# Two column blocks of w2 in sixteen small early transfers, w2's end in parts of 4, 3 and 1, and a reordered head: a decode block of attention beside a Mish layer on one core

## The chip, the cores and the metric

The kernel runs on one core of a Trainium2 chip. The metric is the device time of one execution in microseconds (us), as the median of several executions. A profile is taken from one execution; its "span" reaches from the first to the last recorded instruction and is a little shorter than the execution's own time. The core has five engines with a queue of instructions each: TensorE (PE, with its weight loads as PEld), VectorE (DVE), ScalarE (ACT), GpSimd (POOL) and SyncE (SP). Transfers between HBM and the on-chip memory SBUF are issued by SP or by ACT and carried by 16 DMA engines.

## The reference

One decode step for 8 sequences (B = 8) of width D = 512. After a layer norm, grouped-query attention with 32 query heads on 8 key/value heads over a cache of 8192 positions, and a dense layer with Mish of width F = 1792, are computed side by side and added to the input:

```python
xn = _layernorm(x)
q = (xn @ wq)                      # 8 x 32 heads x 128
scores = q . k_cache * 128**-0.5   # cache: 8 x 8 x 8192 x 128, float32
o = softmax(scores) . v_cache
h = xn @ w1 + b1
act = h * tanh(softplus(h))
out = x + o @ wo + act @ w2
```

Everything is float32. The two caches are 268 MB each, so the execution reads 561 MB.

## The kernel before

**Units.** The work is cut into 32 units (`UNITS`); a unit is one sequence and two key/value heads. Each unit needs one transfer of 8.4 MB from the key cache (`k_t`, laid out as `kT`) and one of 8.4 MB from the value cache (`v_t`). Eight units with the same pair of heads make a group; wq comes in four parts of 2 MB, one per group, into the tile `ws`.

**Places in SBUF.** One tile `kv` of 160 KB per partition holds everything large: values at `V_AT`, keys alternately at the two places `K_AT`. Before the first keys arrive in the first key place, x, its centred copy `xc`, the bias b1 and some small tiles lie there, and w1 is loaded into that place. After the last unit wo (four parts) and w2 take the place of the values and the keys.

**The order.** All instructions are first recorded in a `Program`; `solve` finds which must wait for which, and `emit` writes them out. Every engine runs its own in the order of the source. PE and DVE run units 1 to 30 as a loop of 15 turns with two units each; SP, ACT and POOL are written out without a loop. All large transfers are issued by SP, one after the other; x and b1 alone are issued by ACT. A transfer that PE waits for has its own semaphore.

**The head.** DVE first clears four PSUM banks (H, O, M, A) and makes the small selection matrices (`perm`, `gsum`, `mask` and so on), and only then the layer norm of x. PE multiplies x into bank A, transposes `xc` (four pieces) and the reordered copy `xd` (eight pieces) into bank M. When they are done, SP issues w1 and then the second unit's keys. `project(0, ...)` then multiplies by wq in two halves of eight matmul instructions, each followed by a copy on ACT and four transposes on PE.

**The end.** `parts` cuts w2, seen as 128 rows of 56 column blocks (a block is 512 B of a row), into six transfers: 16, 16, 8, 8, 6 and 2 blocks. PE takes the four parts of wo (`outputs`), the first two parts of w2 (`down_wide`, into bank A) and the others block by block (`down`, into bank H); ACT copies A between, PE adds it to H, DVE copies H to `os`, and SP stores it.

```python
w2_rows = w2.rearrange("j p f -> (j p) f").rearrange("(q i) f -> q (i f)", i=W2R)
parts = ((0, 16), (16, 32), (32, 40), (40, 48), (48, 54), (54, 56))
for lo, hi in parts:
    t = kv[:, W2_AT + lo * P : W2_AT + hi * P]
    nc.sync.dma_start(t, w2_rows[:, lo * P : hi * P])
```

Of the kernel before, what the change touches and what calls it, by code (L numbers as in the profile page):

```python
# [14 lines left out]
P = 128  # L15
B = 8
# [9 lines left out]
G = 4  # L26
# [37 lines left out]


LOAD_Q, MAKE_Q, SPREAD_Q = 4, 5, 7

FIRST, TURNS = 1, (UNITS - 2) // 2
HEAD = mybir.EngineType.DVE
# [356 lines left out]
def kernel(  # L426
# [94 lines left out]
    make_identity(nc, ident)  # L521
    nc.gpsimd.memset(ones, 1.0)
    nc.gpsimd.memset(pt8, 0.0)
    for t in (H, O, M, A):
        nc.vector.memset(t, 0.0)
    for d in range(2):
        nc.vector.tensor_copy(
            perm.rearrange("p (d k c h) -> p d k c h", d=2, c=2, h=REP)[:, d],
# [2 lines left out]
    nc.vector.reduce_sum(  # L531
        gsum, ident.rearrange("p (x g q) -> p g x q", g=4, q=PP), axis=AX.XY
    )
    nc.vector.reduce_sum(mask, ident.rearrange("p (x d) -> p x d", x=NB), axis=AX.X)
    nc.vector.reduce_sum(bsel, ident.rearrange("p (g q) -> p q g", g=G), axis=AX.X)
    nc.vector.reduce_sum(
        isel, ident.rearrange("p (c t h) -> p t c h", t=TL, h=H2), axis=AX.XY
# [1 line left out]
    for d in range(2):  # L539
# [2 lines left out]
            ident.rearrange("p (c d k h) -> p d h c k", c=2, d=2, h=REP)[:, d],  # L542
            axis=AX.XY,
        )
    nc.vector.reduce_sum(
        wide[:, 0], ident.rearrange("p (g i) -> p g i", g=DG), axis=AX.X
    )
    nc.vector.tensor_copy(
        wide[:, 1:], wide[:, 0:1].to_broadcast([P, NB - 1, DG])
    )  # L550
    nc.vector.reduce_sum(dsel, ident.rearrange("p (g i) -> p i g", i=DI), axis=AX.X)
    nc.vector.reduce_sum(
        fsel, ident.rearrange("p (c h g) -> p h c g", h=2, g=2 * W1R), axis=AX.XY
    )
    nc.vector.reduce_sum(usel, ident.rearrange("p (q i) -> p i q", i=WOR), axis=AX.X)
    nc.vector.reduce_sum(
        qsel[:, :Q], ident.rearrange("p (q i) -> p q i", i=WOR), axis=AX.X
# [9 lines left out]
        .to_broadcast([G, 2, 2, B]),  # L567
    )


    st = const.tile([B, 8], F32, name="st")
    nc.vector.reduce_sum(st[:, 0:1], x_sb, axis=AX.X)
    nc.vector.tensor_scalar_mul(st[:, 1:2], st[:, 0:1], 1.0 / D)
    nc.vector.tensor_scalar(xc, x_sb, st[:, 1:2], None, op0=ALU.subtract)
    nc.scalar.activation(sq, xc, AF.Square, accum_out=st[:, 2:3])
    nc.vector.tensor_scalar(
        st[:, 3:4], st[:, 2:3], 1.0 / D, EPS, op0=ALU.mult, op1=ALU.add
    )
    nc.scalar.activation(st[:, 4:5], st[:, 3:4], AF.Sqrt)
    nc.vector.reciprocal(st[:, 5:6], st[:, 4:5])  # L580
    nc.vector.tensor_mul(st[:, 6:7], st[:, 5:6], st[:, 5:6])
    nc.vector.tensor_mul(st[:, 7:8], st[:, 6:7], st[:, 3:4])
    nc.vector.tensor_scalar(st[:, 6:7], st[:, 7:8], -0.5, 1.5, op0=ALU.mult, op1=ALU.add)
    nc.vector.tensor_mul(st[:, 4:5], st[:, 6:7], st[:, 5:6])
    nc.vector.tensor_scalar(xc, xc, st[:, 4:5], None, op0=ALU.mult)
    nc.tensor.matmul(A[:B, :], ident[:B, :B], x_sb, start=True, stop=False)
    for c in range(CC):
        nc.tensor.transpose(M[:, c * B : (c + 1) * B], xc[:, c::CC], ident[:B, :B])
    nc.vector.tensor_copy(xn4.rearrange("p c b -> p (c b)"), M[:, 0:32])
    xd = kv[:B, W1_AT + 3 * D : W1_AT + 5 * D].rearrange("p (i k) -> p i k", i=W1R)  # L590
    for h in range(2):
        nc.vector.tensor_copy(
            xd.rearrange("p i (c h g) -> p h i c g", c=CC, h=2)[:, h],
            xc.rearrange("p (c g i) -> p i c g", c=CC, i=W1R),
        )
    for i in range(W1R):
        nc.tensor.transpose(
            M[:, 32 + i * B : 32 + (i + 1) * B], xd[:, i], ident[:B, :B]
        )
    for h in range(2):  # L600
        nc.vector.tensor_scalar(
            xnT[:, :, h],
            M[:, 32 : 32 + W1R * B].rearrange("p (i b) -> p i b", i=W1R),
            fsel[:, h : h + 1],
            None,
            op0=ALU.mult,
        )

    def project(m, qp):

        nc.tensor.take("wq")
        w = ws.rearrange("p (c f) -> p c f", c=CC)
        for d in range(2):
            for c in range(CC):
                nc.tensor.matmul(
                    H[:B, :],
                    xn4[:, c, :],
                    w[:, c, d * 512 : (d + 1) * 512],
                    start=(c == 0),
                    stop=(c == CC - 1),  # L620
                )
            nc.scalar.copy(qp[:B], H[:B]).tell("qp")
            nc.tensor.take("qp")
            for h in range(REP):
                at = 192 + (d * REP + h) * B
                made = nc.tensor.transpose(
                    M[:, at : at + B], qp[:B, h * DH : (h + 1) * DH], ident[:B, :B]
                )
        made.tell("tq")
        qT = ws[:, 2 * BW : 2 * BW + H2 * B]  # L630
        nc.vector.take("tq")
        nc.vector.tensor_scalar_mul(qT, M[:, 192 : 192 + H2 * B], DH**-0.5).tell("q")
        return qT
# [64 lines left out]
        if part == 1:  # L698
            made.tell("s")

    def softmax(j):
        nc.vector.take("s")
        nc.vector.relay()
        nc.vector.tensor_reduce(nm, S, axis=AX.X, op=ALU.max, negate=True).tell("nm")
        nc.tensor.take("nm")
        nc.tensor.transpose(M[:1, 0:P], nm, ident).tell("mt")
        nc.vector.take("mt")
        row = M[:1, 0:P].rearrange("p (c d k h) -> p d h c k", c=2, d=2, h=REP)
        for d in range(2):
            low_max = nc.vector.tensor_reduce(nr[:, d], row[:, d], axis=AX.XY, op=ALU.min)  # L710
        low_max.tell("nr")
        nc.vector.take("nr")
        for c in range(2):
            wide_max = nc.vector.tensor_copy(
                nx[:, c],
                nr.rearrange("p d (o h) -> p d o h", o=1).to_broadcast([1, 2, NH * G, REP]),
            )
        wide_max.tell("nx")
        nc.tensor.take("nx")
        nc.tensor.transpose(  # L720
            M[:, 128:129], nx.rearrange("p c d k h -> p (c d k h)"), ident[:1, :1]
        ).tell("xt")
        nc.vector.take("xt")
        nc.vector.tensor_copy(nmx, M[:, 128:129])
        nc.scalar.activation(es[j % 2], S, AF.Exp, bias=nmx, accum_out=l).tell("e")
# [97 lines left out]

    hp = H[:, :FG]

    def hidden(w1_t, b1_sb):
        for i in range(W1R):
            for n in range(2):
                nc.tensor.matmul(
                    hp[Q * n : Q * n + 2 * B, :],  # L830
                    xnT[:, i].rearrange("p h b -> p (h b)"),
                    w1_t[:, i, n * FG : (n + 1) * FG],
                    start=(i == 0),
                    stop=False,
                )
        for n in range(2):
# [96 lines left out]
    def down(lo, hi, w):  # L933
        for n in range(lo, hi):
            j, g = divmod(n, G)
            nc.tensor.matmul(
                H[Q * g : Q * g + B, :P],
                aT[:, j, :],
                w[:, (n - lo) * P : (n - lo + 1) * P],
                start=(n < parts[2][0] + G),  # L940
                stop=(j == 2 * W2R - 1),
            )


    nc.sync.dma_start(
        kv[:, W1_AT : W1_AT + W1R * W1F],
        w1.rearrange("j p f -> (j p f)").rearrange("(p f) -> p f", p=P),
    )
    qT = project(0, es[0])
    k_t[1] = load_unit(kT, 1, K_AT[1])  # L950
    mask_queries(qT)
    spread()
    key_weights(0)

    w2_rows = w2.rearrange("j p f -> (j p) f").rearrange("(q i) f -> q (i f)", i=W2R)
    v_t = {}
    for j in range(UNITS):
        b = j % B
# [16 lines left out]
        softmax(j)  # L975
        if b == 0 and j > 0:
            with nc.only("sums"):
                sums()
# [15 lines left out]
            load_q(j // B + 1)  # L994
        if more and b == MAKE_Q:
            with nc.only("make"):
                qT = project(j // B + 1, es[(j + 1) % 2])
                mask_queries(qT)
        turn(j, late)
        if j == 0:  # L1000
            hidden(w1_t, b1_sb)
        if j > 0:
            merge(j - 1)
    sums()
    nc.turn = None

# [7 lines left out]
            .rearrange("(p f) -> p f", p=P),  # L1014
        )
    w2_t = []
    parts = ((0, 16), (16, 32), (32, 40), (40, 48), (48, 54), (54, 56))
    for lo, hi in parts:
        t = kv[:, W2_AT + lo * P : W2_AT + hi * P]
        nc.sync.dma_start(t, w2_rows[:, lo * P : hi * P])  # L1020
# [6 lines left out]
    turn_masked(NP - 1, es[0])  # L1027
    turn_rows(NP - 1)
    outputs(NP - 1, w_o[NP - 1])
    down_wide(*parts[0], w2_t[0])  # L1030
    down_wide(*parts[1], w2_t[1])
    down(*parts[2], w2_t[2])
# [58 lines left out]
```

## Time and profile before

| | us |
|---|---|
| median of 3 executions | 1303.69 (1303.64 to 1304.04) |
| the profiled execution | 1303.81 |
| its span | 1302.0 |
| PE busy | 912.2 (70%) |
| DVE busy | 399.5 (31%) |
| ACT busy | 43.1 (3%) |
| queue of SP's transfers, share of 16 DMA engines | 99.6% |

How the page is read: the busy time of an engine is a mean over the whole execution. The line called DMA cuts the span into 40 slices and gives the busy share of the 16 DMA engines in tenths (9 is 90% or more). The chain of waits goes back from the last instruction to what released it. A view by windows gives the same sums for stretches that one chooses, and the list of DMA queues can be asked for any stretch, down to one that holds a single packet; its last number is the time that the packets starting there took, as a share of 16 engines over that stretch. It can be above 100% where packets reach beyond the stretch.

### The profile page before, as it was taken

The numbers are of one execution on the slowest core, as the hardware profiler recorded it, in microseconds if no ns is written. First come the engines' busy times: TensorE is split into PE (matmuls) and PEld (weight loads), VectorE is DVE, ScalarE is ACT, GpSimd is POOL, SyncE is SP. The second block draws the span as 40 slices with busy tenths as digits, with TensorE's granted clock in tenths as the row PEclk, the third lists the DMA queues.
The fourth block names the chain that finished last, engine by engine and source line by source line (L and its number), as shares of the span: only waits on it lengthen the run. The fifth ranks groups of instructions, "written<-read, shape, count | busy, mean of one in ns | idle before, by whom it ended". The sixth has DMA issues, their size and how long they took to land. (4 is left out here: it accounts for less than half of the span.)

```text
span 1302.0 us, 11473 instructions
## 1 busy us (share of the span) xinstructions
PE 912.2 (70%) x4570; PEld 297.8 (23%) x4570; DVE 399.5 (31%) x874; ACT 43.1 (3%) x104; POOL 1.7 (0%) x8
## 2 busy tenths in 40 slices
PE   4877767668766668775678666677576667666667
PEld 1222222222222222222222222222222222222121
DVE  3332233431333331233321333322333331333431
ACT  2000000000000000000000000000000000000000
POOL 0000000000000000000000000000000000000000
PEclk9899778898788788888887877798887798788788
DMA  9999999999999999999999999999999999999998
GB/s 400 452 422 441 427 437 433 435 433 431 439 427 443 425 445 425 443 425 445 425 443 427 443 427 441 429 435 433 433 437 433 435 429 441 427 443 425 443 418 351
DMA packets 11555, 561.22 MB, mean 431 GB/s; under 512 B 1292, under 2 KB 1552, under 8 KB 1944
## 3 DMA queue, kind: packets, MB, share of 16 engines
q1 hardware_dynamic: 11520, 561.06, 99.6%
q8 instruction: 6, 0.10, 0.0%
q14 instruction: 5, 0.04, 0.0%
q10 hardware_dynamic: 24, 0.02, 0.0%
HBM read 561.01 MB, written 0.07 MB: 431 GB/s over the span
## 5 line engine op out<-in xcount | busy, mean ns | idle before, releaser
L378 PE MATMUL s<-kv,wk 128*64 128x512 f32 x2048 | 515.7, 667 | 226.2 <-PEq L365 226.2
L378 PEld LDWEIGHTS s<-kv,wk 128*64 128x64 f32 x2048 | 174.5, 154 | 550.0 <-issue 550.0
L378 PE MATMUL o<-kv,pt 128*32 128x512 f32 x2048 | 268.1, 683 | 22.7 <-PEq L365 22.3
L378 DVE TENSOR_REDUCE nm<-s 128x1 f32<-128x512 f32 x32 | 22.1, 692 | 479.5 <-DVEq L365 479.5
L378 PEld LDWEIGHTS o<-kv,pt 128*32 128x32 f32 x2048 | 81.5, 123 | 183.1 <-issue 182.7
L378 DVE TENSOR_SCALAR os<-o,isel 128x128 f32<-128x128 f32 x32 | 11.2, 351 | 287.7 <-DVEq L365 287.7
L378 DVE STREAM_TRANSPOSE tr<-x 128x512 f32<-128x512 f32 x128 | 80.0, 682 | 1.3 <-DVEq L365 1.3
L378 DVE TENSOR_TENSOR wk<-qr,mask 128x512 f32<-128x512 f32 x64 | 61.8, 1007 | 8.9 <-DVEq L365 6.4
L378 DVE SCALAR_TENSOR_TENSOR pt<-tr,gsum,y 64x256 f32<-64x256 f32 x128 | 56.2, 479 | 5.2
L378 ACT ACTIVATE e<-s,nmx 128x512 f32<-128x512 f32 x32 | 22.0, 687 | 1046.1 <-DVE nmx L378 1046.1
L378 DVE SCALAR_TENSOR_TENSOR y<-tr,gsum,y 128x512 f32<-128x512 f32 x64 | 48.3, 755 | 9.4
L378 DVE SCALAR_TENSOR_TENSOR os<-o,isel,os 128x128 f32<-128x128 f32 x96 | 33.7, 351 | 14.1 <-DVEq L365 0.3
L378 PE MATMUL x<-e,perm 128*128 128x512 f32 x64 | 36.5, 653 | 1.4 <-PEq L365 1.3
L378 PE MATMUL m<-ident,nm 128*1 128x128 f32 x32 | 8.6, 269 | 32.2 <-PEq L365 32.2
L378 PE MATMUL h<-ws,xn 128*8 128x512 f32 x64 | 30.5, 622 | 0.0
L378 PE MATMUL m<-ident,nx 1*128 1x1 f32 x32 | 6.4, 200 | 34.2 <-PEq L365 34.2
L378 PE MATMUL t<-ident,os 128*128 128x128 f32 x32 | 9.6, 299 | 26.6 <-PEq L365 26.6
L378 DVE TENSOR_SCALAR y<-tr,gsum 128x512 f32<-128x512 f32 x32 | 24.1, 754 | 1.2
L378 DVE TENSOR_REDUCE nr<-m 1x4 f32<-1x64 f32 x64 | 11.0, 207 | 18.1 <-DVEq L365 18.1
L378 PEld LDWEIGHTS m<-ident,nm 128*1 128x1 f32 x32 | 2.5, 79 | 59.5 <-issue 59.5
L378 PEld LDWEIGHTS x<-e,perm 128*128 128x128 f32 x64 | 10.0, 192 | 24.1 <-issue 23.7
L378 PEld LDWEIGHTS t<-ident,os 128*128 128x128 f32 x32 | 4.5, 140 | 46.6 <-issue 46.6
(91 smaller groups left out, 154.1 us busy)
## 6 DMA issues: line engine op xcount, KB each, us to landing
ws<-in_wq SPq DMA_DIRECT2D x4, 2048.0 KB, 32.6
kv<-in_wo SPq DMA_DIRECT2D x4, 2048.0 KB, 24.4
kv<-in_w SPq DMA_DIRECT2D x1, 3584.0 KB, 22.0
kv<-in_w SPq DMA_DIRECT2D x2, 1024.0 KB, 32.0
kv<-in_w SPq DMA_DIRECT2D x2, 512.0 KB, 33.8
kv<-in_kT SPq DMA_DIRECT2D x32, 29.1
kv<-in_v SPq DMA_DIRECT2D x32, 29.4
kv<-in_w SPq DMA_DIRECT2D x1, 384.0 KB, 34.7
```

Of the source, the lines that this page charges most:

```text
L378: ins = getattr(engine, op.method)(*[here(x) for x in op.args], **{k: here(x) for k, x in op.kw.items()})
```

## The change

1. In units 24 to 31, after `merge`, ACT issues two small transfers per unit, 16 in all. They carry blocks 32 and 33 of w2 (1 KB per row) into a free part of `ws`, in 15, 14, ... 1 and at last 8 rows. PE takes these two blocks in a `down` of its own ahead of the first `down_wide`.
2. The parts of w2 at the end are now 16, 16, 6, 8, 4, 3 and 1 blocks.
3. The head is reordered. The layer norm comes ahead of most selection matrices, with a first activation that has ACT load the table for the square root; the transposes of `xd` (now `turn_x`, into bank X) stand inside `project(0, ...)`, between its matmuls and its transposes; the two halves of wq's product use two banks and two tiles; x is multiplied into bank A after `project`; and `hidden` (the product with w1) is spread over the first unit's softmax. SP's w1 transfer stands behind all of `project(0, ...)` and behind the matmul into A. A `project` in the loop keeps its order.

```diff
+EARLY = (32, 34)
+EARLY_ROWS = tuple(range(15, 0, -1)) + (8,)
+EARLY_AT = UNITS - B
...
-    for t in (H, O, M, A):
-        nc.vector.memset(t, 0.0)
+    st = const.tile([B, 8], F32, name="st")
+    nc.scalar.activation(st[:, 0:1], ident[:B, :1], AF.Sqrt)
+    nc.vector.memset(M, 0.0)
+    nc.vector.reduce_sum(st[:, 0:1], x_sb, axis=AX.X)
...
-    def project(m, qp):
+    def project(m, qps, banks, fill=None):
...
+        products(0)
+        if fill is not None:
+            products(1)
+            fill()
+            turned(0)
+        else:
+            turned(0)
+            products(1)
+        turned(1).tell("tq")
...
-                start=(n < parts[2][0] + G),
+                start=(n < EARLY[0] + G),
...
+    def turn_x():
+        for i in range(W1R):
+            nc.tensor.transpose(X[:, i * B : (i + 1) * B], xd[:, i], ident[:B, :B])
...
+    qT = project(0, es, (H, Y), turn_x)
+    nc.tensor.matmul(A[:B, :], ident[:B, :B], x_sb, start=True, stop=False)
     nc.sync.dma_start(
         kv[:, W1_AT : W1_AT + W1R * W1F],
         w1.rearrange("j p f -> (j p f)").rearrange("(p f) -> p f", p=P),
     )
-    qT = project(0, es[0])
...
+    w2_early = ws[:, 3 * BW : 3 * BW + (EARLY[1] - EARLY[0]) * P]
...
+        if j == 0:
+            softmax(j, hidden)
+            hidden(4, 6)
+        else:
+            softmax(j)
...
+        if j >= EARLY_AT:
+            for n in range(2 * (j - EARLY_AT), 2 * (j - EARLY_AT + 1)):
+                rows = slice(sum(EARLY_ROWS[:n]), sum(EARLY_ROWS[: n + 1]))
+                nc.scalar.dma_start(w2_early[rows], w2_rows[rows, EARLY[0] * P : EARLY[1] * P])
...
-    parts = ((0, 16), (16, 32), (32, 40), (40, 48), (48, 54), (54, 56))
+    parts = ((0, 16), (16, 32), (34, 40), (40, 48), (48, 52), (52, 55), (55, 56))
...
+    down(*EARLY, w2_early)
     down_wide(*parts[0], w2_t[0])
```

More of the change, by code (lines that the diff above doesn't have):

```diff
@@ L523 @@
     nc.gpsimd.memset(pt8, 0.0)
-    for t in (H, O, M, A):
-        nc.vector.memset(t, 0.0)
+    st = const.tile([B, 8], F32, name="st")
+    nc.scalar.activation(st[:, 0:1], ident[:B, :1], AF.Sqrt)
+    nc.vector.memset(M, 0.0)
+    nc.vector.reduce_sum(st[:, 0:1], x_sb, axis=AX.X)
+    nc.vector.tensor_scalar_mul(st[:, 1:2], st[:, 0:1], 1.0 / D)
+    nc.vector.tensor_scalar(xc, x_sb, st[:, 1:2], None, op0=ALU.subtract)
+    nc.scalar.activation(sq, xc, AF.Square, accum_out=st[:, 2:3])
+    nc.vector.memset(H, 0.0)
+    nc.vector.reduce_sum(dsel, ident.rearrange("p (g i) -> p i g", i=DI), axis=AX.X)
+    nc.vector.tensor_scalar(
+        st[:, 3:4], st[:, 2:3], 1.0 / D, EPS, op0=ALU.mult, op1=ALU.add
+    )
+    nc.scalar.activation(st[:, 4:5], st[:, 3:4], AF.Sqrt)
+    nc.vector.reduce_sum(
+        wide[:, 0], ident.rearrange("p (g i) -> p g i", g=DG), axis=AX.X
+    )
+    nc.vector.reciprocal(st[:, 5:6], st[:, 4:5])
+    nc.vector.tensor_mul(st[:, 6:7], st[:, 5:6], st[:, 5:6])
+    nc.vector.tensor_mul(st[:, 7:8], st[:, 6:7], st[:, 3:4])
+    nc.vector.tensor_scalar(st[:, 6:7], st[:, 7:8], -0.5, 1.5, op0=ALU.mult, op1=ALU.add)
+    nc.vector.tensor_mul(st[:, 4:5], st[:, 6:7], st[:, 5:6])
+    nc.vector.tensor_scalar(xc, xc, st[:, 4:5], None, op0=ALU.mult)
+    for c in range(CC):
+        nc.tensor.transpose(M[:, c * B : (c + 1) * B], xc[:, c::CC], ident[:B, :B])
+    nc.vector.tensor_copy(xn4.rearrange("p c b -> p (c b)"), M[:, 0:32])
+    nc.vector.tensor_copy(
+        wide[:, 1:], wide[:, 0:1].to_broadcast([P, NB - 1, DG])
+    )
+    nc.vector.reduce_sum(mask, ident.rearrange("p (x d) -> p x d", x=NB), axis=AX.X)
+    xd = kv[:B, W1_AT + 3 * D : W1_AT + 5 * D].rearrange("p (i k) -> p i k", i=W1R)
+    for h in range(2):
+        nc.vector.tensor_copy(
+            xd.rearrange("p i (c h g) -> p h i c g", c=CC, h=2)[:, h],
+            xc.rearrange("p (c g i) -> p i c g", c=CC, i=W1R),
+        )
+    nc.vector.reduce_sum(
+        fsel, ident.rearrange("p (c h g) -> p h c g", h=2, g=2 * W1R), axis=AX.XY
+    )
+    nc.vector.memset(A, 0.0)
+    nc.vector.memset(O, 0.0)
     for d in range(2):
@@ L533 @@
     )
-    nc.vector.reduce_sum(mask, ident.rearrange("p (x d) -> p x d", x=NB), axis=AX.X)
     nc.vector.reduce_sum(bsel, ident.rearrange("p (g q) -> p q g", g=G), axis=AX.X)
@@ L544 @@
         )
[L545 to L554, printed above, removed]
     nc.vector.reduce_sum(usel, ident.rearrange("p (q i) -> p i q", i=WOR), axis=AX.X)
@@ L568, with products @@
     )
[L571 to L607, printed above, removed]
-    def project(m, qp):
+    def project(m, qps, banks, fill=None):
         nc.tensor.take("wq")
         w = ws.rearrange("p (c f) -> p c f", c=CC)
-        for d in range(2):
+        def products(d):
             for c in range(CC):
                 nc.tensor.matmul(
-                    H[:B, :],
+                    banks[d][:B, :],
                     xn4[:, c, :],
@@ L621, in project, with turned @@
                 )
-            nc.scalar.copy(qp[:B], H[:B]).tell("qp")
+            nc.scalar.copy(qps[d][:B], banks[d][:B]).tell("qp")
+        def turned(d):
             nc.tensor.take("qp")
@@ L626, in project @@
                 made = nc.tensor.transpose(
-                    M[:, at : at + B], qp[:B, h * DH : (h + 1) * DH], ident[:B, :B]
+                    M[:, at : at + B], qps[d][:B, h * DH : (h + 1) * DH], ident[:B, :B]
                 )
-        made.tell("tq")
+            return made
+        products(0)
[7 more added lines that the diff above has]
+        turned(1).tell("tq")
         qT = ws[:, 2 * BW : 2 * BW + H2 * B]
@@ L699, in scores, with softmax @@
             made.tell("s")
-    def softmax(j):
+    def softmax(j, fill=lambda lo, hi: None):
         nc.vector.take("s")
@@ L704, in softmax @@
         nc.vector.tensor_reduce(nm, S, axis=AX.X, op=ALU.max, negate=True).tell("nm")
+        fill(0, 2)
         nc.tensor.take("nm")
@@ L718, in softmax @@
         wide_max.tell("nx")
+        fill(2, 4)
         nc.tensor.take("nx")
@@ L824, with hidden @@
     hp = H[:, :FG]
-    def hidden(w1_t, b1_sb):
-        for i in range(W1R):
+    def hidden(lo, hi):
+        for i in range(lo, hi):
             for n in range(2):
@@ L835, in hidden @@
                 )
+        if hi < W1R:
+            return
         for n in range(2):
@@ L939, in down @@
                 w[:, (n - lo) * P : (n - lo + 1) * P],
-                start=(n < parts[2][0] + G),
+                start=(n < EARLY[0] + G),
                 stop=(j == 2 * W2R - 1),
             )
+    def turn_x():
+        for i in range(W1R):
+            nc.tensor.transpose(X[:, i * B : (i + 1) * B], xd[:, i], ident[:B, :B])
+        for h in range(2):
+            nc.vector.tensor_scalar(
+                xnT[:, :, h],
+                X[:, : W1R * B].rearrange("p (i b) -> p i b", i=W1R),
+                fsel[:, h : h + 1],
+                None,
+                op0=ALU.mult,
+            )
+    qT = project(0, es, (H, Y), turn_x)
+    nc.tensor.matmul(A[:B, :], ident[:B, :B], x_sb, start=True, stop=False)
     nc.sync.dma_start(
@@ L974 @@
         scores(j, k, j % 2 == 0, 1)
-        softmax(j)
+        if j == 0:
[3 more added lines that the diff above has]
+            softmax(j)
         if b == 0 and j > 0:
@@ L996 @@
             with nc.only("make"):
-                qT = project(j // B + 1, es[(j + 1) % 2])
+                qT = project(j // B + 1, [es[(j + 1) % 2]] * 2, (H, H))
                 mask_queries(qT)
@@ L1000 @@
         if j == 0:
-            hidden(w1_t, b1_sb)
+            hidden(6, W1R)
         if j > 0:
             merge(j - 1)
+        if j >= EARLY_AT:
+            for n in range(2 * (j - EARLY_AT), 2 * (j - EARLY_AT + 1)):
+                rows = slice(sum(EARLY_ROWS[:n]), sum(EARLY_ROWS[: n + 1]))
+                nc.scalar.dma_start(w2_early[rows], w2_rows[rows, EARLY[0] * P : EARLY[1] * P])
     sums()
```

## The prediction

> **What bounds the kernel now.** I read the page first, for what is busy from end to end; then the chain of waits, for what ends last; then windows over the last microseconds.
>
> ```profile
> span 1302.0 us, 11473 instructions
> ...
> DMA  9999999999999999999999999999999999999998
> ...
> q1 hardware_dynamic: 11520, 561.06, 99.6%
> ```
>
> ```profile
> 1263.61 34.75 DMA kv<-in_w
> ...
> 1298.40 0.74 PE h L378 x15
> ...
> 1299.16 0.29 DVE os L378
> ```
>
> The 16 DMA engines are full in every slice, 99.6% of the span by SP's queue alone. The last instruction hangs on w2's last transfer, which lands at 1298.35. So the time is: start, plus the bytes of the DMA engine that ends last over its rate, plus what follows the landing. An edit counts only if it leaves the DMA engines dry, changes the load of the engine that ends last, or shortens what follows.
>
> ```profile
> 2.00:26.00 24.00, 13.08 (x38) 3.67 (x38) 8.73 (x36) 4.46 (x7) 0.70 (x1) 1.00 1.04 436
> 60.00:1250.00 1190.00, 838.13 (x4173) 276.37 (x4169) 367.62 (x793) 33.11 (x85) 0.00 (x0) 0.84 1.00 434
> 1297.00:1297.56 0.56, 0.23 (x11) 0.13 (x11) 0.00 (x0) 0.00 (x0) 0.00 (x0) 1.00 0.15 57
> 1297.56:1298.01 0.45, 0.45 (x16) 0.20 (x8) 0.00 (x0) 0.00 (x0) 0.00 (x0) 1.00 0.05 20
> 1298.01:1298.36 0.35, 0.04 (x4) 0.00 (x0) 0.00 (x0) 0.00 (x0) 0.00 (x0) 1.00 0.07 23
> ```
>
> The last two columns are the DMA engines' busy share and GB/s. The rate is 434 to 436 GB/s in the head and in the long middle: there is no hole to fill. At the end the engines stop one by one: 0.15 x 16 = 2.4 are at work until 1297.56, and from there on 0.05 x 16 = 0.8 and 0.07 x 16 = 1.1, so **one engine alone** for the last 0.8 us. That straggler sets the end.
>
> **The change, part by part.** First the price of a packet (one row of a transfer on one DMA engine).
>
> ```profile
> q10 hardware_dynamic: 4, 0.01, 3.7%
> q1 hardware_dynamic: 8, 0.01, 6.0%
> q1 hardware_dynamic: 1, 0.07, 1511.2%
> ```
>
> These are rows of the list of DMA queues, asked for three stretches in turn. In 5.80 to 6.30 ACT's queue brings b1: 4 packets of 1.8 KB, 0.037 x 16 x 0.5 = 0.30 us, 0.074 each. In 1298.015 to 1298.36 the straggler works alone on seven rows of 1 KB and a word that counts the transfer: 0.06 x 16 x 0.345 = 0.331 us, about 0.046 a row and 0.009 the word. In 60.17 to 60.18 one key packet of 65,536 B starts: 15.112 x 16 x 0.01 = 2.418 us, 0.0378 per KB. So a packet takes 0.008 + 0.0378 per KB: 0.159 for 4 KB, 0.121 for 3, 0.084 for 2, 0.065 for 1.5, 0.046 for 1, 0.027 for 0.5.
>
> *Removed and added at the end.* Each engine carries 8 of the 128 rows. Before, the parts of 8, 6 and 2 blocks cost it 8 x (0.159 + 0.121 + 0.046) = 2.61 us. After, 6, 4, 3 and 1 blocks cost 8 x (0.121 + 0.084 + 0.065 + 0.027) + 0.01 for one more count = 2.39. **Term 1: -0.22 us** on every engine alike.
>
> *Added before.* These bytes still have to come, and in units 24 to 31 the engines are as full as ever (434 GB/s), so a packet there delays all that its engine carries later. What matters is who gets them.
>
> ```profile
> q1 hardware_dynamic: 11, 0.18, 184.8%
> q10 hardware_dynamic: 16, 0.02, 9.6%
> ```
>
> This is 1.80 to 2.30. x has 8 rows and shows as 16 packets of ACT's queue, 8 rows and 8 counts: one row each on 8 engines; b1's 4 rows are the 4 packets above. I take it that a transfer of n rows goes one row each to n engines, always the same first ones: numbered so, engine i gets 15 - i rows from the falling lengths, and one more from the 8 if i is below 8. That is 16 rows for engine 0 and none for engine 15, each with its count 0.055 us: **term 2 between +0.88 and 0**, on the straggler by its number. So I need the number. The packets of an engine follow each other end to start, which lets the straggler's be followed back from its last one. Near the front end of that chain stands a packet of b1 (the first row below, the one packet of ACT's queue that starts in 6.18 to 6.20). From 6.26 on three packets of wq (0.61) lead to 8.09, eight of keys (2.415) to 27.4, eight of w1 (1.06) to 35.9 and ten more of keys to 60.03, where an instruction fetch falls on the same engine:
>
> ```profile
> q10 hardware_dynamic: 1, 0.00, 23.1%
> q14 instruction: 1, 0.01, 1.9%
> q1 hardware_dynamic: 1, 0.07, 1845.6%
> ```
>
> In 60 to 61 that fetch of 8 KB takes 0.019 x 16 = 0.30 us, and the key packet behind it (60.33 to 60.34) 18.456 x 0.16 = 2.953, that is 0.54 over the usual 2.418. A fetch at 1252.47 with the same row (asked for 1252 to 1253) falls on it too, and one near 70.5: so it is late. An engine with a row of b1 is one of the first four, with 16 to 13 early rows: +0.88 to +0.72. I take **+0.80**, and keep 0 as the other end, for the chain is read from packets some of which lie within 0.01 us of each other.
>
> In the Trainium skill, "DMA: Bandwidth & Descriptors", section "Why a DMA increments its semaphore by 16 and not by 1", says that a transfer issued so uses the largest k up to 16 that divides its rows, on the lowest-numbered k engines. The counts of x and b1 agree; that the low numbers are always taken, no row here can show. By that rule term 2 stands as it is.
>
> *After the landing.* Today four matmuls (two blocks) wait for the last transfer, then two. The 16 matmuls at 1298.40 spread over 0.74 us with 0.27 for a single one, so 0.03 each: **term 3: -0.06**, with -0.12 and 0 as its ends.
>
> ```profile
> L378 PE MATMUL h<-kv,aT x48: 272/273/276, 1296.2 to 1298.8; 128*8 128x128 f32 x48
> 80.42 0.13 PEld L378 LDWEIGHTS m<-ident,nx 1*128 1x128 f32 x1 [1.26 <-issue]
> 80.72 0.19 PEld L378 LDWEIGHTS o<-kv,pt 128*32 128x32 f32 x8 [0.17 <-issue]
> 1292.52 0.18 PEld L378 LDWEIGHTS a<-kv,aT 128*8 128x8 f32 x4 [0.68 <-DMA kv<-in_w]
> 1298.40 0.42 PEld L378 LDWEIGHTS h<-kv,aT 128*8 128x8 f32 x16 [0.63 <-DMA kv<-in_w]
> ```
>
> *Waits on PE.* The new `down` must wait for 16 transfers that landed long before. At 80.42 to 80.72 PE passed two waits (values, probabilities) in 0.30 us, 0.15 each at most; 16 make 0 to 2.4 us, ahead of `down_wide`, `down`, ACT's copy of A, and the store. PE stands idle for w2 just there (0.68 and 0.63 in the rows), so I cost it at nothing; without that cover it would be the 2.4.
>
> ```profile
> 0.90 0.59 ACTq L378 DMA_DIRECT2D kv<-in_x  x1
> 1.53 0.26 ACTq L378 DMA_DIRECT2D kv<-in_b  x1
> L378 ACT ACTIVATE e<-s,nmx 128x512 f32<-128x512 f32 x32 | 22.0, 687 | 1046.1 <-DVE nmx L378 1046.1
> ```
>
> *Issue on ACT.* Sixteen issues, at 0.26 to 0.59 us as for b1 and x, two per unit, behind that unit's exponential. ACT idles 1046.1/32 = 33 us ahead of each exponential: nothing. SP's seventh part of w2 joins a queue that holds 30 us of work: nothing.
>
> *The head.* SP's w1 transfer, and the keys behind it, now wait for all of `project(0)` and the matmul into A.
>
> ```profile
> 0.95 0.38 SPq L378 DMA_DIRECT2D ws<-in_wq  x1
> 1.39 0.42 SPq L378 DMA_DIRECT2D kv<-in_kT  x1
> 3.29 1.87 PE L378 MATMUL a<-kv,ident 8*8 8x512 f32 x2 [3.29 <-DVE a L378]
> 13.35 1.02 PE L378 MATMUL m<-ident,kv 8*128 8x8 f32 x8 [1.33 <-DVE kv L378]
> 14.29 5.33 PE L378 MATMUL h<-ws,xn 128*8 128x512 f32 x8
> 20.69 3.60 PE L378 MATMUL h<-ws,xn 128*8 128x512 f32 x8
> DMA to landing us min/median/max: 24.8/26.5/41.7
> DMA to landing us min/median/max: 7.6/32.6/32.7
> ```
>
> The last two rows are the shortest, middle and longest time to landing of the keys up to 80 us and of wq. The first keys, issued at 1.39, land 24.8 later, at 26.2: until then the queue is fed. wq, issued at 0.95, lands 7.6 later, at 8.6, and the layer norm, moved up by over 5 us, no longer holds the product back. From 8.6: 5.33 + 3.60 for 16 matmuls, 1.02 for `turn_x`, about 1 for the transposes, 1.87 for A: 20.4. Even with all 16 at the slow pace (10.7) it is 22.2. From SP's issue at 0.95 to 11 packets of wq in 1.80 to 2.30 it is at most 1.4 us, so w1 is there by 21.8 to 23.6, ahead of 26.2. **Term 4: 0.** The first unit's scores start some 5 us sooner, which a full queue does not pass on.
>
> **The sum.** -0.22 + 0.80 - 0.06 = +0.5 us, with -0.3 for a straggler at number 15 and +0.7 for number 0. Against the profiled execution (1303.81; 1.8 of it lies outside its span) that is 1304.3; against the median, 0.12 lower, 1304.2. A measurement here can tell about 0.2%, 2.6 us, from no change: this is a fifth of it.
>
> **The rivals.** *Another straggler (the engines level out).* If the straggler is a high number, or other code lengths move its fetches, terms 1 and 3 are left, and at best the 0.8 us that it works alone: 1302.9 to 1303.4. For it: the fetches depend on the code, and the code changes. Against: the chain to b1. Chance 0.28.
>
> *Slower: a small packet costs more than its bytes.* Each early packet breaks into a stream of 65,536 B packets, as a fetch does, and the packet behind a fetch took 0.54 longer. At that price a first-four engine pays 13 to 16 times 0.055 + 0.54, 7.7 to 9.5 us: 1311 to 1313. It decides the sign by my bound from (2.6 + 0.3)/16 - 0.055 = 0.13 us per packet. Against it: b1's packets came between wq's of 16,384 B, and the one behind it took as long as one with none before it:
>
> ```profile
> q1 hardware_dynamic: 1, 0.02, 381.9%
> ```
>
> (This row answers for 5.93 to 5.94, behind a packet of b1, and word for word for 4.74 to 4.75, where none is near: 3.819 x 0.16 = 0.611.) Chance 0.06. The Trainium skill's page "DMA: Bandwidth & Descriptors", section "Rules for kernel authors", speaks against the change in the same sense: coalesce small transfers, for under 64 KB one pays mostly overhead. With that page's fixed 2.0 us each, all on the path, 16 would make an estimated 32 us. By b1's row the engine pays 0.074 and no more.
>
> *PE ends last.* The 16 waits push PE past the landing: up to 2.4 less the idle time, I say +0.5 to +1.5 in all: 1304.3 to 1305.2. Chance 0.09.
>
> *The small transfers are split in another way* (all rows of one on a single engine, say): 16 x 0.055 spread otherwise, within the same bounds; or the head leaves a hole after all, 1 to 3 us. Together 0.04.
>
> **How the numbers follow.** Forecast 0.53: 1304.2, itself between 1303.7 and 1304.6. The levelling rival (0.28) reaches down to 1302.9, PE up to 1305.2; the executions shown differ by 0.4. The range 1303.0 to 1305.1 leaves out the slower rival, a hole, and the edges. Beyond 2.6 us slower lies only the packet rival and part of a hole, 0.07; faster by as much nothing that I can name, since the DMA engines have no hole: 0.01; within it 0.92.
>
> **What would show it.** DMA shares at 9 in all slices and 434 GB/s in the middle; w1 issued near 20; the straggler's last packet near 1298.9; two matmuls behind the last landing. A key packet beside an early one of 2.4 us rather than 2.95 refutes the slower rival. A queue run dry before 27 us, or w1 issued after 25, would break term 4; another engine last would break term 2.

## The result and the profile after

The changed kernel takes 1322.0 us, the median of four executions that lie far apart (1318.09, 1307.69, 1326.33 and 1325.91), against 1303.74 before. The ratio is 1.0121, with a 95% interval from 1.0082 to 1.016: slower, clear of the noise. The prediction was 1304.2 with a range up to 1305.1. The profiled execution of the changed kernel is the one of 1318.09. Here and in the table of experiments, medians count every execution, while the ratios leave out the slow ones, which are those over 1.5% above the fastest of their kernel (one each of e7, e16 and e18).

First the lines of its page that answer to those of before, and the last steps of its chain of waits (start, us, engine):

```profile
span 1316.3 us, 11498 instructions
...
DMA  9999999999999999999999999999999999999998
GB/s 403 439 441 423 440 424 431 452 422 438 444 422 440 424 440 440 424 438 442 426 438 424 440 440 424 438 442 426 438 423 439 423 413 407 425 438 388 401 389 344
...
q1 hardware_dynamic: 11664, 560.93, 99.6%
q10 hardware_dynamic: 280, 0.16, 0.0%
```

```profile
1282.90 29.86 DMA kv<-in_w
...
1312.80 0.59 PE h L383 x8
...
1313.42 0.29 DVE os L383
```

The chain ends as before: w2's last transfer lands, PE takes what is left, DVE copies. The DMA line is the same to the digit, and SP's queue still occupies 99.6%. Only the GB/s line differs: from the 33rd slice on (a slice is 32.9 us) it falls to 413, 407 and, after two normal slices, to 388, 401 and 389. **The DMA engines are as busy as before and move less.** A busy share cannot show this, since a packet that takes longer is busy for longer.

The early transfers start at 983 us. So I cut the span there, by windows; the columns of interest are the last two, DMA share and GB/s. Before:

```profile
60.00:980.00 920.00, 654.20 (x3239) 215.51 (x3235) 278.60 (x600) 26.46 (x66) 0.00 (x0) 0.85 1.00 434
985.00:1280.00 295.00, 200.13 (x1050) 65.59 (x1046) 97.84 (x212) 6.64 (x19) 0.00 (x0) 0.83 1.00 433
```

After:

```profile
60.00:980.00 920.00, 644.11 (x3217) 214.10 (x3216) 275.90 (x594) 27.16 (x68) 0.00 (x0) 0.85 1.00 434
985.00:1280.00 295.00, 191.10 (x956) 62.66 (x948) 95.03 (x206) 6.64 (x19) 0.00 (x0) 0.82 1.00 414
1045.00:1066.00 21.00, 17.98 (x114) 6.21 (x110) 1.83 (x7) 0.78 (x2) 0.00 (x0) 1.00 1.03 447
1072.00:1099.00 27.00, 17.11 (x66) 5.91 (x66) 5.67 (x14) 0.78 (x2) 0.00 (x0) 0.75 1.01 388
1112.00:1140.00 28.00, 16.59 (x67) 5.67 (x66) 10.06 (x21) 0.38 (x1) 0.00 (x0) 0.82 1.00 433
1190.00:1220.00 30.00, 16.64 (x67) 5.78 (x67) 10.25 (x21) 0.78 (x2) 0.00 (x0) 0.83 1.00 384
1249.00:1265.00 16.00, 13.01 (x62) 4.37 (x62) 2.84 (x10) 0.78 (x2) 0.00 (x0) 0.89 1.02 443
```

Ahead of the first early transfer nothing has changed, 434 GB/s. From there to 1280 us it is 414 for 433, and 295 x (433 - 414) / 433 = 12.9 us of the 14.3 by which the span has grown. The loss is not spread evenly. It comes in stretches: full speed, then 388, full speed again, 384, full speed. (In windows this short the GB/s count a packet where it starts, so 433 to 447 is all full speed.) Outside these windows lie two more, a short one at the start and one at the end, which single packets show below.

The list of DMA queues tells what a single packet does. A key or value packet of 65,536 B takes 2.418 us before, and one that starts in 1120.09 to 1120.10 of the changed kernel takes just that. In 1080.21 to 1080.22, inside a slow stretch, and in 985.59 to 985.60, right behind the first early transfer, the rows are:

```profile
q1 hardware_dynamic: 1, 0.07, 1696.2%
...
q1 hardware_dynamic: 1, 0.07, 1742.5%
```

16.962 x 16 x 0.01 = 2.714 us, and 2.788. The stretch at the start is over with the second early transfer: a packet that starts in 993.53 to 993.54 takes 2.418 again. At the end, one that starts in 1275.69 to 1275.70 takes 2.789. The packets of all 16 engines take so long in such a stretch, those of engines that got no early row too: in 1073.00 to 1075.72, a little over the time of one such packet, 16 packets start, one for each engine, and their mean is 0.998 x 2.72 = 2.715 us.

```profile
q1 hardware_dynamic: 16, 1.05, 99.8%
```

The slow stretch of 1072 sets in with the sixth early transfer (10 rows and a count, asked for 1066 to 1069):

```profile
q10 hardware_dynamic: 11, 0.01, 1.0%
```

0.010 x 16 x 3 = 0.48 us for 11 packets, 0.044 each. **The early packets themselves are as cheap as predicted, and all the others become slower**, by 0.30 us in 2.418, for some 35 us after the small packets are through.

What ends a slow stretch is not always another small transfer. The one that holds at 1200 to 1243 (390 GB/s) ends where none is near, at an instruction fetch of 16 KB that takes 0.017 x 16 x 4 = 1.1 us; these are the two rows for 1245 to 1249 and the window before (the one behind, from 1249, stands above with 443):

```profile
q1 hardware_dynamic: 26, 1.70, 104.5%
q8 instruction: 1, 0.02, 1.7%
1200.00:1243.00 43.00, 27.73 (x135) 8.76 (x133) 11.79 (x26) 0.78 (x2) 0.00 (x0) 0.82 1.00 390
```

It is no rule: in e15 below, a packet takes 2.714 us before such a fetch (in 1268.41 to 1268.42, the fetch at 1272.44) and one behind it as well (in 1277.72 to 1277.73).

### The profile page after: what moved, and what is told of

It reads as the page before. It is cut to its first block, busy times and chain, and to the rows that moved or that the text cites. A ratio compares the mean times of both kernels' runs of the same rounds, so it can differ in the third digit from the quotient of the medians.

```text
span 1316.3 us, 11498 instructions
## 1 busy us (share of the span) xinstructions
PE 905.6 (69%) x4570; PEld 297.7 (23%) x4570; DVE 399.6 (30%) x874; ACT 42.1 (3%) x104; POOL 1.7 (0%) x8
## 3 DMA queue, kind: packets, MB, share of 16 engines
q1 hardware_dynamic: 11664, 560.93, 99.6%
## 5 line engine op out<-in xcount | busy, mean ns | idle before, releaser
L383 PE MATMUL h<-ws,xn 128*8 128x512 f32 x56 | 26.9, 626 | 0.7 <-PEq L370 0.7
```

The lines of the kernel that those rows point to most:

```text
L383: ins = getattr(engine, op.method)(*[here(x) for x in op.args], **{k: here(x) for k, x in op.kw.items()})
```

## The experiments

All kernels are the changed one with the edit shown, unless told otherwise. Names in capitals are theories. QUEUES: an engine pays for turning between SP's and ACT's queue. SKEW: the small rows delay some of the engines against the others, and the shift does the harm. PLACE: what counts is which partitions the small rows are written to. The others are named where they arise. "Rate" is the GB/s of the window from 985 to 1280 us in the profiled execution, which need not be a middle one: it took 1335.51 us in e7, 1340.86 in e10, 1347.85 in e15 and 1352.15, the slowest, in e16.

| kernel | median us (lowest to highest, executions) | ratio to before [95% interval] | rate |
|---|---|---|---|
| e1_no_early | 1303.67 (1303.51 to 1304.36, 10) | 1.0 [0.9991, 1.001] | 432 |
| e7_old_head | 1322.16 (1317.35 to 1340.99, 5) | 1.011 [1.009, 1.013] | 393 |
| e2_early_sp | 1321.43 (1316.36 to 1327.43, 4) | 1.0131 [1.0091, 1.0171] | 406 |
| e4_one128 | 1303.72 (1303.57 to 1304.07, 10) | 1.0 [0.999, 1.0009] | 433 |
| e6_once | 1305.12 (1304.79 to 1305.41, 10) | 1.001 [1.0001, 1.002] | |
| e5_scan | 1310.06 (1309.88 to 1310.1, 3) | 1.0048 [1.0031, 1.0065] | 430 |
| e3_8x16 | 1312.9 (1311.57 to 1317.68, 4) | 1.0077 [1.0053, 1.01] | 418 |
| e9_row0 | 1311.94 (1311.32 to 1315.98, 4) | 1.0073 [1.0056, 1.009] | 423 |
| e8_cycle | 1333.03 (1328.46 to 1337.6, 2) | 1.0224 [1.0184, 1.0265] | 433 |
| e11_8_row0 | 1304.64 (1304.37 to 1304.74, 10) | 1.0006 [0.9996, 1.0015] | 433 |
| e13_8_row64 | 1304.51 (1304.36 to 1304.7, 10) | 1.0007 [0.9998, 1.0016] | 432 |
| e14_8_row56 | 1304.61 (1304.32 to 1304.89, 10) | 1.0007 [0.9998, 1.0017] | 432 |
| e18_8_row104 | 1304.6 (1304.49 to 3469.03, 10) | 1.0006 [0.9997, 1.0016] | 432 |
| e10_16x8 | 1334.31 (1328.6 to 1340.86, 4) | 1.0219 [1.0186, 1.0253] | 387 |
| e12_own | 1303.7 (1303.57 to 1304.08, 11) | 1.0 [0.9991, 1.0009] | 432 |
| e15_16_row56 | 1353.92 (1347.85 to 1357.86, 4) | 1.0396 [1.038, 1.0412] | 379 |
| e16_src8 | 1343.35 (1330.84 to 1352.15, 4) | 1.0272 [1.0218, 1.0327] | 371 |
| e17_dst8 | 1304.17 (1304.12 to 1304.51, 10) | 1.0004 [0.9994, 1.0013] | 432 |

### Which part of the change costs the time

**e1_no_early**: everything but the early transfers. Blocks 32 and 33 stay in the third part.

```diff
-        if j >= EARLY_AT:
...
-    parts = ((0, 16), (16, 32), (34, 40), (40, 48), (48, 52), (52, 55), (55, 56))
+    parts = ((0, 16), (16, 32), (32, 40), (40, 48), (48, 52), (52, 55), (55, 56))
...
-    down(*EARLY, w2_early)
```

> The changed kernel without the sixteen early transfers: blocks 32 to 40 come in one part again, the rest of the end (4, 3, 1) and the reordered head stay. Theory SKEW (the unequal early rows shift the DMA engines against one another, and some positions of the engines slow all 16) and theory QUEUES (ACT's queue beside SP's on the same engines slows them): 1303.2 to 1304.2, no key or value packet above 2.42 us but those behind an instruction fetch. Theory HEAD (the new order of the head or other code is at fault) or OUTSIDE (something beyond this core): 1307 to 1326 again.

1303.67, no difference from before. So the head and the cut of w2's end together cost and bring nothing that can be measured.

**e7_old_head**: the kernel before, with the early transfers, their `down` and the new parts alone.

```diff
+        if j >= EARLY_AT:
+            for n in range(2 * (j - EARLY_AT), 2 * (j - EARLY_AT + 1)):
...
-    parts = ((0, 16), (16, 32), (32, 40), (40, 48), (48, 54), (54, 56))
+    parts = ((0, 16), (16, 32), (34, 40), (40, 48), (48, 52), (52, 55), (55, 56))
...
+    down(*EARLY, w2_early)
```

> The kernel before with only the sixteen early transfers and the new parts of the end, its old head kept. SKEW: slow stretches from unit 24 on as in the changed kernel, 1307 to 1326. If the new head is needed too: 1303.5 to 1304.7.

1322.16, the same loss without the new head. With e1 this puts the whole of it on the early transfers.

**e2_early_sp**: SP issues the 16 early transfers.

```diff
-                nc.scalar.dma_start(w2_early[rows], w2_rows[rows, EARLY[0] * P : EARLY[1] * P])
+                nc.sync.dma_start(w2_early[rows], w2_rows[rows, EARLY[0] * P : EARLY[1] * P])
```

> The sixteen early transfers as they are (15, 14, ... 1 and 8 rows), but issued by SP, in the one queue with the keys and values. SKEW: the same shifts, so slow stretches as in the changed kernel, 1307 to 1326. QUEUES: only one queue is at work, so 1303.5 to 1304.7.

1321.43, rate 406: QUEUES falls, for now all packets are of one queue and the loss stays. It also clears ACT's issuing.

**e4_one128**: the two blocks come early in one transfer of all 128 rows.

```diff
-EARLY_ROWS = tuple(range(15, 0, -1)) + (8,)
+EARLY_ROWS = (128,)
...
-            for n in range(2 * (j - EARLY_AT), 2 * (j - EARLY_AT + 1)):
+            for n in range(j - EARLY_AT, int(j == EARLY_AT)):
```

> The same two blocks in one early transfer of 128 rows on ACT's queue in unit 24, 8 rows for every DMA engine. SKEW: all engines are delayed alike by 8 x 0.05 us, no shift: 1303.3 to 1304.3. QUEUES: a stretch of about 7 us at 12% less, and more if the state stays: 1304.5 to 1326.

1303.72, rate 433. The same bytes at the start of the same stretch do no harm, as 8 rows for each engine. So it is the cut into small transfers.

### Shift or place

**e6_once** and **e5_scan** test SKEW on 8 rows. In place of the early transfers, e6 has one transfer of 8 rows of 12 KB in unit 9, and e5 has 24 transfers of 8 rows of 2.5 KB, one in nearly every unit, which move half of the engines against the others step by step through a whole packet time. The data is read by nobody, and blocks 32 and 33 come at the end again, as in all kernels below whose small data is not used. The line is e6's:

```diff
+        if j == 9:
+            nc.scalar.dma_start(ws[:8, :3072], w2_rows[:8, :3072])
```

> The kernel without early transfers, with a single transfer of 8 rows of 12 KB on ACT's queue in unit 9 (data that nothing uses): the first eight DMA engines fall 0.46 us behind the others once, as after some ten of e3's transfers, where its slow stretch began. SKEW: slow packets (above 2.6 us) from then on for many units, with no other small transfer near: 1310 to 1410. STEPS: a disturbance of some 40 us at 12%, then 2.42 us again: 1304 to 1309.

> The kernel without early transfers, with one transfer of 8 rows of 2.5 KB (data that nothing uses) on ACT's queue in each of 24 units: each moves the first eight DMA engines about 0.10 us further behind the other eight, in all about one packet (2.4 us). SKEW: the packets of all 16 engines change their duration at these transfers and hold it between them, slow over some ranges of the shift and 2.42 us over others; 1306 (only the 24 rows) plus a slow part, 1310 to 1400. The rival that remains, STEPS (each such transfer disturbs for a while, wherever the engines stand): a slow stretch after each of the 24, alike.

While e6's transfer is under way the rate falls (375 GB/s in 404 to 413), and then it is at once the usual one, here from 415 us to 980:

```profile
404.00:413.00 9.00, 3.28 (x9) 1.46 (x11) 7.27 (x14) 0.81 (x4) 0.00 (x0) 0.54 0.97 375
415.00:980.00 565.00, 402.71 (x1979) 133.27 (x1975) 167.39 (x358) 16.34 (x40) 0.00 (x0) 0.84 1.00 434
```

These 9 us cost 9 x (434 - 375) / 434 = 1.2 of the 1.45 us that e6 is over e1. A lasting slow stretch, as SKEW had it, or one of some 40 us, as STEPS had it, is not there. In e5 the rate is 434 from 60 us to 640, 433 from there to 980 and 430 to 1280: no shift brings a lasting slow stretch. Its time, 6.4 us over e1's, lies at the edge of what SKEW gave, so it is the rate that speaks against SKEW here. The rows explain 24 x (0.008 + 0.0378 x 2.5) = 2.5 us of the 6.4 on the engines that get them; the rest was not looked into.

**e3_8x16** brings the two blocks in sixteen transfers of 8 rows, rows 8n to 8n + 7. **e10_16x8** brings them in eight transfers of 16 neighbouring rows, one for every engine, so that no engine is shifted against another. The lines are e10's:

```diff
-EARLY_ROWS = tuple(range(15, 0, -1)) + (8,)
+EARLY_ROWS = (16,) * 8
...
-            for n in range(2 * (j - EARLY_AT), 2 * (j - EARLY_AT + 1)):
+            for n in range(j - EARLY_AT, j - EARLY_AT + 1):
```

> Sixteen early transfers on ACT's queue, each of 8 rows, so that the first eight DMA engines get 16 rows each and the others none. SKEW: the two halves move against each other by up to 16 x 0.05 = 0.8 us but within a half nothing moves: other slow stretches than in the changed kernel, or none, 1303.7 to 1326. QUEUES: as many stretches with both queues at work, slow as before, 1307 to 1326.

> The two blocks in eight early transfers of 16 rows on ACT's queue, one per unit from 24 on: every DMA engine gets one row of each, so the engines are not moved against each other, but a row's place in SBUF is not the engine's own part (the large transfers give each engine 8 rows of its own). SKEW: 1303.3 to 1304.3 and no slow packets. Theory PLACE (a small row written into the partitions that another engine is filling leaves that path slow until something lets it drain): slow stretches, 1306 to 1326.

e10 takes 1334.31, more than the change itself, with no shift at all: SKEW falls. In windows of it between its first and second, second and fourth, and fourth and fifth early transfer:

```profile
988.00:1043.00 55.00, 27.77 (x137) 9.02 (x136) 17.82 (x38) 1.59 (x6) 0.00 (x0) 0.79 0.99 349
1050.00:1108.00 58.00, 40.63 (x203) 13.99 (x205) 13.05 (x31) 1.56 (x4) 0.00 (x0) 0.88 1.00 434
1115.00:1151.00 36.00, 19.97 (x85) 6.66 (x77) 11.65 (x25) 0.78 (x2) 0.00 (x0) 0.79 1.01 350
```

The first transfer brings the rate down, the second brings it back, the third changes nothing, the fourth brings it down again. Between two transfers the rate stands still. e3 is slow only late: 434 GB/s from 985 to 1140 us and 384 from 1185 to 1215.

**e9_row0**, **e11_8_row0** and **e8_cycle** ask for the place. e9 keeps the change's lengths (15, 14, ... 1 and 8 rows), but all from partition 0 on. e11 has sixteen transfers of 8 rows, all on partitions 0 to 7. e8 has 24 transfers of the same 8 rows of w2 from unit 1 on, written to partitions 0 to 7, 8 to 15 and so on up to 127, and then from 0 again. The data is read by nobody. The lines are e8's:

```diff
+            lo = 8 * (len(smalls) % 16)
+            smalls.append(nc.scalar.dma_start(ws[lo : lo + 8, 3 * BW : 3 * BW + 256], w2_rows[:8, :256]))
```

> The changed kernel's sixteen lengths (15, 14, ... 1 and 8 rows, units 24 to 31), but each begins at row 0, so they write partitions 0 to 14 alone; the data is not used, and blocks 32 to 40 come at the end in one part. SKEW: the engines are moved exactly as in the changed kernel: slow stretches, 1307 to 1326. PLACE: only the partitions of a few engines are touched: 1303.7 to 1305, or slow where a transfer reaches beyond row 7.

> As e3 (sixteen transfers of 8 rows) but each on rows 0 to 7, with data that is not used. SKEW: the same movement of the halves as in e3, so the same slow stretches, 1310 to 1318. PLACE: as in e5 no lasting slow stretch, 1303.7 to 1305.

> One transfer of 8 rows of 1 KB in each of 24 units (always the same rows of w2, not used), into partitions 0 to 7, 8 to 15, ... 120 to 127 and again 0 to 63. SKEW: slow ranges, if any, follow the shift of 0.05 us per transfer, whatever the partitions. PLACE: slow stretches begin at some of the places, above all from partition 64 on, and not at 0 to 7.

e11 against e3: as many transfers, rows and bytes, 1304.64 for 1312.9. So the place decides (e3 also reads other rows each time, e11 always the same; e8 rules the rows out). e8 reads the same rows throughout and is slow in a stretch of its own, between 642 and 806 us; its windows:

```profile
440.00:640.00 200.00, 142.70 (x694) 47.28 (x694) 60.34 (x130) 6.21 (x14) 0.00 (x0) 0.85 1.00 434
645.00:671.00 26.00, 17.46 (x68) 6.26 (x68) 5.60 (x14) 0.78 (x2) 0.00 (x0) 0.76 1.00 358
675.00:734.00 59.00, 35.19 (x186) 10.99 (x178) 18.80 (x39) 1.59 (x6) 0.00 (x0) 0.82 1.00 374
764.00:804.00 40.00, 23.17 (x117) 7.43 (x109) 11.57 (x25) 0.78 (x2) 0.00 (x0) 0.84 1.01 364
810.00:980.00 170.00, 119.98 (x611) 39.32 (x603) 51.92 (x110) 5.43 (x12) 0.00 (x0) 0.86 1.00 435
```

Its first ten transfers (partitions 0 to 79) do nothing. The eleventh, on 80 to 87, brings the rate down; the next three, up to 111, change its level, and the fifteenth, on 112 to 119, brings it back. In e9 the first transfer, 15 rows on partitions 0 to 14, brings it down (393 GB/s in 998 to 1040), and from 1050 us to 1280 the rate is 432 again, though all its later transfers lie on partitions 0 to 11. So neither a low place nor a small transfer as such is the rule.

### Which place

**e12_own** is e10 with one line changed: transfer n brings rows n, n + 8, ..., n + 120 instead of 16 neighbours. If a transfer of 128 rows gives every engine eight neighbouring rows (no row of the trace names the engine of a packet), each early row then goes to an engine that writes this partition anyway. No run shows which partitions an engine writes, nor that row i of a small transfer goes to engine i; HALF and OWN below count engines and partitions by this assumption.

```diff
-                rows = slice(sum(EARLY_ROWS[:n]), sum(EARLY_ROWS[: n + 1]))
+                rows = slice(n, P, 8)
```

**e13_8_row64** and **e14_8_row56** are e11 on partitions 64 to 71 and 56 to 63, and **e15_16_row56** has eight transfers of 16 rows, all on 56 to 71.

> [...] HALF (a small packet does harm where one of the engines 0 to 7 writes a partition of the upper 64, or one of 8 to 15 a partition of the lower 64): no crossing, so 1303.5 to 1304.3, and no stretch in which the 64-KB packets take over 2.45 us. OWN (harm where an engine writes a partition that another engine writes in the large transfers, in either half): the same. Neither (each small transfer of 16 packets harms wherever it lies): over 1320 again.

> Sixteen transfers of 8 rows as in the version with rows 0 to 7 (1304.64 us), now all on partitions 64 to 71, with data that nobody reads. HALF: each of them crosses, engines 0 to 7 into the upper 64 partitions: 1308 to 1330, with stretches in which all 64-KB packets take 2.65 us or more. OWN: in both versions at most one of the eight engines writes a partition of its own, so about 1304.6 as there, or, if rows 0 to 7 were an exception, slow in the next version as well.

> The same on partitions 56 to 63. HALF: no crossing, 1304.4 to 1304.9 as with rows 0 to 7, no slow stretch. [...]

> [...] HALF: 1303.5 to 1304.3, no slow stretch. OWN: over 1310, as with 16 neighbouring rows elsewhere (1334.31).

e12 takes 1303.7: the change's two blocks come early, in as many packets as in e10, and nothing is lost. Its packets behind the first transfer run at full rate where e10 had 349:

```profile
988.00:1043.00 55.00, 33.28 (x164) 11.53 (x158) 22.36 (x46) 1.59 (x6) 0.00 (x0) 0.81 1.00 433
```

HALF falls on two sides: e13, which it had slow, takes 1304.51, and e15, which it had at full speed, is the slowest kernel of all, 1353.92. OWN gives e12 and e15. But by the same assumption all 8 rows of a transfer in e13, and 7 of 8 in e14, are written to partitions of other engines, and they do no harm there. With another assignment of partitions to engines OWN would give other cases; that was not tested.

**e16_src8** and **e17_dst8** take e12 apart, which differs from e10 in the rows read as well as in the partitions written. The first line below is e16's, the second e17's. **e18_8_row104** is e11 on partitions 104 to 111, where e8 had been slow.

```diff
+                smalls.append(nc.scalar.dma_start(ws[56 : 72, 3 * BW : 3 * BW + 256], w2_rows[n::8, 4096:4352]))
```

```diff
+                smalls.append(nc.scalar.dma_start(ws[n::8, 3 * BW : 3 * BW + 256], w2_rows[: 16, 4096:4352]))
```

> As the eight transfers of 16 rows on partitions 56 to 71 (1353.92 us), but transfer k reads rows k, k+8, ..., k+120 of w2 in place of rows 0 to 15; the data is read by nobody. The version that reads and writes k, k+8, ..., k+120 took 1303.7. DESTINATION (the partitions that the small rows are written to decide): still over 1320, with stretches of 64-KB packets over 2.65 us. SOURCE (the rows that are read decide): 1303.5 to 1304.3, and no such stretch.

> The other half of the pair: eight transfers of 16 rows that read rows 0 to 15 of w2 each time and write partitions k, k+8, ..., k+120. DESTINATION: 1303.5 to 1304.3 and no slow stretch. SOURCE: over 1320.

> Sixteen transfers of 8 rows, all on partitions 104 to 111. On 0 to 7, 56 to 63 and 64 to 71 the time was 1304.5 to 1304.6 with no slow stretch; in the version whose 8-row transfers cycle through the partitions, stretches of slow packets began at partitions 80 to 111. PLACE (each pair of engine and partition is harmless or harmful by itself, the harmful ones of the engines 0 to 7 lying at 80 and above): 1308 to 1330, with slow stretches. MOVING (8-row transfers do harm where the place changes from one to the next): 1304.4 to 1304.9 as on the other three places.

DESTINATION holds, by the same window of e16 and then of e17:

```profile
988.00:1043.00 55.00, 30.60 (x150) 9.61 (x142) 16.44 (x35) 0.78 (x2) 0.00 (x0) 0.78 1.00 344
```

```profile
988.00:1043.00 55.00, 35.28 (x160) 11.39 (x154) 22.34 (x46) 1.59 (x6) 0.00 (x0) 0.78 1.00 433
```

Sixteen neighbouring partitions are harmful with either source (e15, e16), and sixteen that lie 8 apart are harmless with either (e12, e17). e18 takes 1304.6 (one of its ten executions took 3469.03, for a reason that nothing here shows; the others 1304.49 to 1304.71), so PLACE as worded there falls for 104 to 111. It does not settle MOVING: in e8 the rate was already low when a transfer came to these partitions, and it had fallen at 80 to 87, where no fixed place was tried.

**What is shown**: the loss comes from the small early transfers; it depends on the partitions that they write, and not on the queue, the source rows, the head, or a shift between the engines. **What stays open** is the rule of the place: 128 rows and 16 rows 8 apart never did harm, 8 rows on one of four fixed places never did, 15 or 16 neighbouring rows did with the first transfer (e9 and the changed kernel, e10, e15, e16), and 8 neighbouring rows did while the place moved on through the partitions.

Why the loss of rate outlives its cause is a guess. The DMA share is 1.00 all the time, so what is held up on a way that several engines share may find no gap to drain. The Trainium skill, "DMA: Bandwidth & Descriptors", section "Back-pressure in remote DMA", describes such a thing for transfers between cores: a destination port of SBUF that is saturated clogs the way back to the sending engines and to others that share it. That several engines slow down together agrees with the 2.714 us of all 16 engines; no run here shows a port, and these transfers are not between cores. That a fetch can end a stretch, while one engine moves 16 KB in 1.1 us in place of a key packet, would fit as well, but was not tested.

## Why the prediction was wrong

**The step that failed** is in "Added before": "in units 24 to 31 the engines are as full as ever (434 GB/s), so a packet there delays all that its engine carries later". From this the prediction took that an early packet costs its own engine its own time, and nobody else anything. Its sum had a term for the load of the engine that ends last and none for the rate at which all 16 run. That rate fell to 414 GB/s on the mean of the stretch, which is 12.9 of the 14.3 us in the profiled execution. With the rate left alone the forecast would have held: e4 and e12, which bring the same blocks early in another way, take 1303.72 and 1303.7.

**Term 2 (+0.80)** had the right price. e11, e13, e14 and e18 put sixteen early packets on each of eight engines at places where the rate stays, and take 0.84 to 0.97 us more than e1: 16 x 0.055 = 0.88 had been worked out. The rows of ACT's queue in the changed kernel give 0.044 a packet. In the change itself it cannot be told from the loss of rate.

**Term 1, the waits on PE, ACT's issues**: right as far as they can be told. e1 does not test term 1, for it leaves both blocks at the end. e12 does, and gives every engine 8 early rows: -0.22 + 8 x 0.055 - 0.06 = +0.16 by the prediction's prices, and 0.04 was measured, against 1303.66 for the kernel before. So small a sum is no sharp test. In the changed kernel PE passes the `down` of the early blocks and then still waits for w2, 1.33 us here and less for the later parts:

```profile
1309.51 0.12 PEld L383 LDWEIGHTS a<-kv,aT 128*8 128x8 f32 x8 [1.33 <-DMA kv<-in_w]
```

**Term 3 (-0.06)** was too small. The work of PE behind the last landing went from 0.74 us to 0.59, by 0.15, past the -0.12 that was its end. The prediction looked for two matmuls there; the profile has 8, as before it had 15 or 16: PE takes the last two parts in one go, and their 4 blocks make 8 matmuls in the trace where the 8 blocks before made 16. In the sum, +0.7 for engine 0 should also have been +0.6 (-0.22 + 0.88 - 0.06). Neither matters beside 14 us.

**Term 4 (0, the head)**: right. SP issues w1 at 19.59, ahead of the 26.2 at which the first keys land, and the first scores start at 27.98:

```profile
19.59 0.33 SPq L383 DMA_DIRECT2D kv<-in_w  x1
...
27.98 2.83 PE L383 MATMUL s<-kv,wk 128*64 128x512 f32 x6 [5.51 <-PEq L370]
```

The full queue does not pass this on, as predicted: e1 gains nothing by it.

**The rival "a small packet costs more than its bytes"** had the sign and a time (1311 to 1313) that is nearer than the forecast, with a chance of 0.06, but another mechanism. It put 0.54 us on the one packet behind each early one, on its own engine. At harmless places the packets behind take nothing more (e12 takes 0.03 us more than e1; e17 takes 0.5, for which its 8 rows on each engine, 8 x 0.055 = 0.44, are enough); at harmful ones all engines pay on every packet for tens of us. Its test, a key packet beside an early one of 2.4 or 2.95 us, was too narrow: the packet at 985.59 took 2.788, and packets far from any early one took 2.714. The evidence against this rival was b1's packet in the head, which is 4 rows on 4 engines. It could not show what 15 rows do, and the prediction had no row for that at all: this unknown was bounded by a fetch of instructions, which disturbs one engine, and should have been bounded also by a common loss of rate.

**The section "Rules for kernel authors" of the Trainium skill's "DMA: Bandwidth & Descriptors"** speaks against small transfers, and here the sign bears it out. The 2 us for each, which the page fits to transfers issued by GpSimd, are not what these cost the kernel: sixteen harmless ones cost 0.84 to 0.97 us in all (e11, e13, e14, e18), and sixteen or eight harmful ones anything from 8 to 50.

## What to carry to other kernels

Where all DMA engines are full, a busy share of 1.00 says nothing of the rate: read GB/s by windows, or the time of a single packet, ahead of and behind each small transfer that is added. A transfer of few rows into a saturated stream can slow all engines for far longer than it lasts; if one is needed, spread its rows over the partitions (all 128, and 16 that lie 8 apart, did no harm here), and time it by itself before anything is built on it. Here that only brings the loss back to nothing: no version was faster than the kernel before, which has no hole to fill.

## What was not expected of the hardware

- Sixteen packets of 1 KB, 0.046 us each (the one in 983.13 to 983.14), lower the rate of all 16 DMA engines from 434 to 349 GB/s for the 55 us up to the next small transfer (e10), and that next one can bring the rate back.
- The lowered rate has levels that hold still. Single packets of 65,536 B take 2.714 us in the changed kernel, 2.956 in e10 (in 1001.02 to 1001.03) and 3.055 in e16 (in 1010.11 to 1010.12):

```profile
q1 hardware_dynamic: 1, 0.07, 1847.5%
```

```profile
q1 hardware_dynamic: 1, 0.07, 1909.4%
```

- Executions of one kernel scatter by 18.6 us in the changed kernel (1307.69 to 1326.33) and by 0.5 to 0.6 at harmless places in e12 and e14. So whether, or how far, a small transfer at a harmful place lowers the rate differs from one execution to the next.
